# Bias loads and the tail of w1 in a two-layer attention and MLP kernel: plain DMAs in place of single elements, 768-byte runs in place of 256-byte ones, and a new table of priorities

## The chip, the cores and the metric

The kernel runs on one core of one Trainium2 chip. The metric is the device time of that core in microseconds (us). A profiled run also has a span, from its first to its last instruction, which is about 2 us shorter than the time; where this document divides a run into sections, they are sections of the span. Every run came with the mean clock that was granted to TensorE; 1.0 is full speed. In the views PE is TensorE, PEld its loading of weights, DVE is VectorE, ACT ScalarE, POOL GpSimd and SP SyncE; an arrow with a name says what an instruction waited for. A DMA is issued by an engine and lands later, when its data is there (b1's load in before: 2.00 us of issue on POOL, landed after 10.2).

## The reference

The program applies an attention mixer and an MLP twice over the same weights. There are 2048 tokens of 576 features, 32 heads of 18, a causal window of 256 keys, and 4608 hidden units.

```python
def _A_ref(x, wqkv, wo):                       # H = 32, Dh = 18, W = 256
    qkv = (x @ wqkv).reshape(B, S, 3, H, Dh)   # transposes cut
    q, k, v = qkv[0], qkv[1], qkv[2]
    scores = jnp.einsum("bhqd,bhkd->bhqk", q, k) * (Dh ** -0.5)
    # mask: key not after the query, and fewer than 256 before it
    p = _softmax(jnp.where(mask[None, None], scores, -1e9), axis=-1)
    return einsum("bhqk,bhkd->bhqd", p, v) ... @ wo

def _B_ref(x, w1, b1, w2, b2):
    y = _layernorm(x, axis=-1)
    h = _gelu(jnp.einsum("bsd,df->bsf", y, w1) + b1)
    return jnp.einsum("bsf,fd->bsd", h, w2) + b2

x = x + _A_ref(_layernorm(x), A_wqkv, A_wo)
x = x + _B_ref(_layernorm(x), B_w1, B_b1, B_w2, B_b2)
# ... and both lines once more
```

## The kernel before

The kernel does not issue instructions in the order of its text. Each operation is added as a task with an engine, what it reads and writes, and an estimated cost; a planner then fixes one order for each engine. A table of numbers by stage (`PL.nudge`) shifts the priorities of the planner. Tokens go in chunks of 512, four chunks in each of two layers. Attention of one chunk is interleaved with the MLP of the one before.

The biases, loaded by GpSimd (POOL) through the software queue:

```python
    b1col = sb("b1col", [P, NF], FP32)
    b2bc = sb("b2bc", [P, D], FP32)
    # ... cut ...
    dma("pool", b2bc[:, :], bass.AP(tensor=B_b2.tensor, offset=B_b2.offset, ap=[[0, P], [1, D]]), reads=["k3"], writes=["b2"], cls="b", ring=2,
        cost=1.0, prio=-1)

    def load_b1(e):
        src = bass.AP(tensor=B_b1.tensor, offset=B_b1.offset, ap=[[1, P], [P, NF], [1, 1]])
        with nc.allow_non_contiguous_dma(reason="bias column layout (init only)"):
            return e.dma_start(b1col[:, :], src)
    add("pool", load_b1, reads=["k3"], writes=["b1"], dma="b", ring=2, cost=2.0, lat=10.0, prio=-1)
```

The load of w1, one group of six column tiles at a time. Its contraction has 576 rows; the last 64 are split over the two halves of the partitions:

```python
        src = B_w1[512:576, cols].rearrange("p (a b f) -> p b a f", a=GS // 2, b=2)
        for b in range(2):
            dma("sp", w1_sb[64 * b:64 * b + 64, sl, 4 * GW:].rearrange("p (a f) -> p a f", a=GS // 2), src[:, b],
                writes=[f"w1b{sl}_{b}"], cls="w1", cost=0.6, lat=1.4, move=0.26, desc=192, prio=prio)
```

And two DMAs. One turns the normalised input of a chunk for the QKV products, on the SP queue; the other, on the POOL queue, brings the residual (the input that is added back later) of one chunk, 1152 KB at a time:

```python
        # in ln_norm_T
        add("sp", lambda e: e.dma_start_transpose(dst[:, :, i * 128:(i + 1) * 128], xn[:, sl, :]),
            reads=rd, writes=[f"{dname}{i}"], dma="t", ring=8, cost=1.3, lat=0.6, move=0.72, desc=640, prio=prio)
    # ... cut ...
    def x_load(a, cnt, reads, prio):
        dma("pool", x_res[:, a:a + cnt, :], x_dram[a * P:(a + cnt) * P, :].rearrange("(t p) d -> p t d", p=P), reads=reads,
            # ... cut ...
            cls="xr", ring=8, cost=1.2, prio=prio)
```

The softmax here doesn't subtract the row's maximum and nothing guards it: scores larger than these inputs give would overflow.

## Time and profile before

| | before |
|---|---|
| time, median of 3 runs | 926.46 us (925.78 to 926.63) |
| profiled run: time, span, granted clock | 925.61 us, 923.8 us, 0.998 |
| first mask of attention on POOL, in the profile | 21.60 us |
| load of the GELU table on ScalarE, ahead of the first MLP | 96.83 us |

The last two rows are milestones. I cut the span at them into a start, a middle and a rest, because the change touches the middle (the biases), all three (w1), and the order of the middle and the rest. For before these three are 21.60, 75.23 and 826.97 us.

The queues over the whole span (packets, MB, and time of packets as a share of 16 engines):

```profile
q1 hardware_dynamic: 212048, 119.90, 53.5%
q0 software_dynamic: 6880, 5.03, 2.9%
```

### The profile page before, as it was taken

What the parts mean: (1) busy time and instruction counts of PE and PEld (TensorE: products, weight loads), DVE (VectorE), ACT (ScalarE), POOL (GpSimd) and SP (SyncE); (2) the same over time, 40 slices, a digit from 0 to 9 for tenths busy, and PEclk for the clock granted to TensorE, in tenths of its full rate; (3) what the DMA queues carried; (4) which work ended last, traced back from release to release, by engine and by line L of the source; (5) the groups of instructions that cost most, each with busy time, mean ns of one, the idle gap of its engine ahead of it and who ended that gap; (6) DMA issues with size and microseconds to landing.
All of it is one profiled execution on the core that took longest, in us unless ns stands there. A gap on an engine that the chain in (4) does not pass through costs nothing. (4 is left out here: it accounts for less than half of the span.)

```text
span 923.8 us, 22403 instructions
## 1 busy us (share of the span) xinstructions
PE 898.5 (97%) x9370; PEld 567.3 (61%) x9408; DVE 319.3 (35%) x796; ACT 599.3 (65%) x721; POOL 372.8 (40%) x507
## 2 busy tenths in 40 slices
PE   8898999999999999999999999999999999999998
PEld 6566465565756657566565657666476665656556
DVE  5657113732317313184124521255123520241001
ACT  5877786677746777563665768646676777852441
POOL 3877353453505535062341644315443353610100
PEclk9999999999999999999999999999999999999999
DMA  7996819743197335852658351873619626175430
GB/s 196 163 226 121 217 57 263 159 138 117 29 244 137 119 114 134 180 103 56 193 77 258 55 192 40 225 142 64 199 40 212 154 71 202 44 201 158 145 116 27
DMA packets 221460, 129.01 MB, mean 140 GB/s; under 512 B 151856, under 2 KB 219184, under 8 KB 221360
## 3 DMA queue, kind: packets, MB, share of 16 engines
q1 hardware_dynamic: 212048, 119.90, 53.5%
q0 software_dynamic: 6880, 5.03, 2.9%
q10 hardware_dynamic: 2432, 2.65, 0.9%
q8 instruction: 74, 1.21, 0.6%
q14 instruction: 26, 0.21, 0.1%
HBM read 91.87 MB, written 2.36 MB: 102 GB/s over the span
## 5 line engine op out<-in xcount | busy, mean ns | idle before, releaser
L765 ACT ACTIVATE pT<-ps 128x1024 bf16<-128x1024 f32 (+2 forms) x384 | 349.3, 969 | 123.8 <-PE ps L756 122.8
L786 POOL TENSOR_SCALAR_AFFINE_SELECT pT<-pT 128x512 bf16<-128x512 bf16 (+1 forms) x368 | 281.7, 790 | 252.0 <-ACT pT L765 226.8
L920 PE MATMUL ps<-w_sb,hT 128*128 128x288 bf16 x2304 | 312.7, 286 | 1.9 <-DVE x_res L837 1.7
L894 ACT ACTIVATE hT<-ps,b1col 128x512 bf16<-128x512 f32 x288 | 198.0, 687 | 170.1 <-PE ps L891 170.1
L891 PE MATMUL ps<-xnTm,w_sb 128*128 128x512 bf16 x1114 | 256.4, 379 | 3.3 <-issue 1.9
L920 PEld LDWEIGHTS ps<-w_sb,hT 128*128 128x128 bf16 x2304 | 212.3, 98 | 74.1 <-issue 17.6
L891 PEld LDWEIGHTS ps<-xnTm,w_sb 128*128 128x128 bf16 x1152 | 108.7, 98 | 135.6 <-issue 17.0
L837 DVE TENSOR_TENSOR x_res<-ps,x_res 128x288 f32<-128x288 f32 x160 | 71.3, 450 | 262.6 <-PE ps L920 221.5
L670 PE MATMUL ps<-wqkv,xnTa 128*128 128x288 bf16 x960 | 136.8, 286 | 2.6 <-DVE qn L709 1.6
L803 PEld LDWEIGHTS ps<-vA,pT 128*128 128x128 bf16 x2880 | 95.1, 96 | 25.7 <-POOL pT L786 8.6
L670 PEld LDWEIGHTS ps<-wqkv,xnTa 128*128 128x128 bf16 x960 | 85.9, 97 | 37.0 <-issue 6.8
L803 PE MATMUL ps<-vA,pT 128*128 128x20 bf16 x2880 | 100.6, 171 | 4.2 <-POOL pT L786 3.3
L709 DVE CAST qn<-ps 128x288 bf16<-128x288 f32 x120 | 54.2, 455 | 100.8 <-PE ps L670 100.4
L902 POOL TENSOR_TENSOR x_res<-x_res,b2bc 128x576 f32<-128x576 f32 x32 | 44.9, 1402 | 104.9 <-ACT hT L894 104.8
L756 PE MATMUL ps<-qT,kT 32*128 32x384 bf16 (+2 forms) x1216 | 64.0, 276 | 3.0 <-ACT pT L765 2.0
L602 POOL TENSOR_SCALAR vtmp<-mv_all 128x1 f32<-128x1 f32 (+1 forms) x43 | 8.9, 207 | 130.8 <-DVE mv_all L593 129.2
L591 DVE BATCH_NORM_STATS2 st_all<-x_res 128x6 f32<-128x288 f32 x104 | 45.1, 449 | 9.3 <-DMA x_res<-in_A_x_dram 7.7
L696 DVE CAST vA<-ps 128x288 bf16<-128x288 f32 x64 | 29.0, 455 | 54.8 <-PE ps L670 54.7
L670 PE MATMUL ps<-wo_sb,attT 128*128 128x288 bf16 x320 | 46.9, 293 | 0.4 <-DMA attT<-attq 0.4
L813 DVE RECIPROCAL rinv<-ps 128x16 f32<-128x16 f32 x64 | 16.2, 254 | 85.0 <-PE ps L803 84.4
L879 PE MATMUL ps<-xnTm,w_sb 64*128 64x512 bf16 x288 | 39.5, 377 | 2.2 <-ACT hT L894 0.9
L614 DVE TENSOR_SCALAR xn<-x_res,mv_all,rstd 128x576 bf16<-128x576 f32 x52 | 36.7, 710 | 11.8 <-DMA xnTm<-xn 6.7
(42 smaller groups left out, 278.2 us busy)
## 6 DMA issues: line engine op xcount, KB each, us to landing
w_sb<-in_B_w_dram SPq DMA_DIRECT2D x48, 864.0 KB, 6.2
w_sb<-in_B_w_dram SPq DMA_DIRECT2D x48, 768.0 KB, 4.8
w_sb<-in_B_w_dram SPq DMA_DIRECT2D x96, 48.0 KB, 4.5
x_res<-in_A_x_dram POOLq DMA_DIRECT2D x4, 1152.0 KB, 8.7
out_dram<-xn SPq DMA_DIRECT2D x16, 144.0 KB, 1.8
wqkv<-in_A_wqkv_dram ACTq DMA_DIRECT2D x3, 576.0 KB, 7.2
hT<-in_A_x_dram SPq DMA_DIRECT2D x2, 576.0 KB, 5.0
wo_sb<-in_A_wo_dram ACTq DMA_DIRECT2D x1, 576.0 KB, 6.3
```

The costliest lines, as they stand in the source:

```text
L591: add("dve", lambda e, i=i, s=s: e.bn_stats(st_all[:, t, i, :], s[:, t, i * HB:(i + 1) * HB]), reads=res, writes=[f"st{t}_{i}"], cost=0.37 ...
L670: ins = e.matmul(bank(bs[o])[:, 0:HB], lhs(c), rhs(c, o * HB), start=(c == 0), stop=(c == KD - 1))
L709: add("dve", lambda e, b=bs[o], dst=dst: e.tensor_copy(dst, bank(b)[:, 0:HB].rearrange("p (h d) -> p h d", d=DH)), reads=[bs[o]], writes=[ ...
L756: ins = e.matmul(two(bs[j // 2])[:, j % 2, col:col + nq * 128], k_of(T0 + so)[0][32 * j:32 * j + 32, g, :], qs[32 * j:32 * j + 32, g, qo * ...
L765: add("act", lambda e, h2=h2: e.activation(pT[:, sl, 2 * h2:2 * h2 + 2, lo:hi], two(bs[h2])[:, :, lo:hi], ACT.Exp, scale=SCALE), reads=[bs ...
L786: add("pool", lambda e, ap=ap, pat=pat, sgn=sgn, kind=kind: e.affine_select(ap, ap, pattern=pat, compare_op=(ALU.is_ge if kind == "d" else ...
L803: ins = e.matmul(bank(B_O)[:, o:o + VW], pT[:, sl, j, col + qi * 128:col + (qi + 1) * 128], vA[:, (T0 + so) % VS, 4 * g + j, :], start=(fi ...
L837: add("dve", lambda e: e.tensor_tensor(x_res[:, t, sl], bank(b)[:, 0:HB], x_res[:, t, sl], ALU.add), reads=[b], writes=[f"x{t}h{hh}"], cos ...
L891: ins = e.matmul(bank(bk)[:, 0:n], w1_sb[:, sl, col:col + 128], xnTm[:, k % 2, c, 0:n], start=False, stop=(c == 3))
L894: add("act", lambda e, ff=ff, fl=fl, bk=bk: e.activation(hT[:, fl, 0:n], bank(bk)[:, 0:n], ACT.Gelu_apprx_tanh, bias=b1col[:, ff:ff + 1]), ...
L902: add("pool", lambda e, t=t: e.tensor_tensor(x_res[:, t, :], x_res[:, t, :], b2bc[:, :], ALU.add), reads=["b2", f"h{fl}"], writes=X(t), co ...
L920: ins = e.matmul(bank(b)[:, 0:HB], hT[:, fl, i * 128:(i + 1) * 128], w2_sb[:, fl, hh * HB:(hh + 1) * HB], start=(fl == 0), stop=(fl == NFH ...
```

## The change

The intent is to spare the DMA engines thousands of tiny packets. b1 comes as 36 rows of 256 bytes, is turned by one TensorE transpose, and is copied to fp32 by VectorE; b2 comes as a plain broadcast, in bf16, without a cast. Both move from POOL to SP. The last 64 rows of w1 come in runs of 768 bytes, where the first three and the last three column tiles take the place of the even and the odd ones. A new table of priorities goes with it.

```diff
-    PL.nudge = {"": -6.61, "ea0": -8.81, "eb0": -4.05, "q1.0": -40.73, ...      # cut
+    PL.nudge = {"b": 1.83, "ea0": -1.98, "ld0+": 40.46, "eb0": 2.23, ...        # cut
-    b2bc = sb("b2bc", [P, D], FP32)
+    b2bc = sb("b2bc", [P, D], BF16)
+    b1in = sb("b1in", [NF, P], BF16)
...
-        src = B_w1[512:576, cols].rearrange("p (a b f) -> p b a f", a=GS // 2, b=2)
         for b in range(2):
-            dma("sp", w1_sb[64 * b:64 * b + 64, sl, 4 * GW:].rearrange("p (a f) -> p a f", a=GS // 2), src[:, b],
-                writes=[f"w1b{sl}_{b}"], cls="w1", cost=0.6, lat=1.4, move=0.26, desc=192, prio=prio)
+            c0 = bb * GW + b * GW // 2
+            dma("sp", w1_sb[64 * b:64 * b + 64, sl, 4 * GW:], B_w1[512:576, c0:c0 + GW // 2], writes=[f"w1b{sl}_{b}"], cls="w1", cost=0.6,
+                lat=1.4, move=0.17, desc=64, prio=prio)
...
-                for ff, sl, bk in zip(fs, sls, bks):
-                    b = ff % 2
-                    col = 4 * GW + ff % GS // 2 * 128
+                for i in (0, 3, 1, 4, 2, 5):
+                    sl, bk = sls[i], bks[i]
+                    b = i // 3
+                    col = 4 * GW + i % 3 * 128
...
-    dma("pool", b2bc[:, :], ...)                                                # cut
-    add("pool", load_b1, reads=["k3"], writes=["b1"], dma="b", ...)             # cut
+    dma("sp", b1in[:, :], bass.AP(tensor=B_b1.tensor, offset=B_b1.offset, ap=[[P, NF], [1, P]]), reads=["k3"], writes=["b1i"], cls="b", ring=2,
+        cost=0.5, prio=-1)
+    dma("sp", b2bc[:, :], bass.AP(tensor=B_b2.tensor, offset=B_b2.offset, ap=[[0, P], [1, D]]), reads=["k3"], writes=["b2"], cls="b", ring=2,
+        cost=0.5, prio=-1)
+    add("pe", lambda e: e.transpose(bank(bb).bitcast(BF16)[:, 0:NF], b1in[:, :], ident[0:NF, 0:NF]), reads=["b1i", "ident"], writes=[bb],
+        cost=0.1, lat=0.22, prio=5, alloc=[bb])
+    add("dve", lambda e: e.tensor_copy(b1col[:, :], bank(bb).bitcast(BF16)[:, 0:NF]), reads=[bb], writes=["b1"], cost=0.1, lat=0.14, prio=5)
```

## The prediction

> **What bounds the kernel now.** I read the page's busy shares first, then the table of stretches (busy time of each engine between two times), then the waits by engine, and last the DMA view of the stretch in which the biases are loaded.
>
> The busy shares say which engine has no room:
>
> ```profile
> PE 898.5 (97%) x9370; PEld 567.3 (61%) x9408; DVE 319.3 (35%) x796; ACT 599.3 (65%) x721; POOL 372.8 (40%) x507
> ```
>
> TensorE (PE) works 898.5 of 923.8 us. Nothing in the change takes away a matmul of the layers, so whatever is gained has to come out of 923.8 - 898.5 = 25.3 us in which TensorE stands still, or from matmuls that run on a lowered clock. Where these lie is told by the stretches (columns: stretch and its length, then PE, PEld, DVE, ACT, POOL, each with its count of instructions, then granted clock, DMA share, GB/s):
>
> ```profile
> 0.00:20.00 20.00, 17.51 (x149) 13.20 (x150) 11.59 (x34) 8.67 (x14) 7.53 (x23) 1.00 0.86 216
> 20.00:30.00 10.00, 9.75 (x122) 7.18 (x119) 6.77 (x21) 8.29 (x12) 7.52 (x9) 1.00 0.65 127
> 30.00:40.00 10.00, 7.78 (x113) 4.77 (x114) 8.22 (x26) 8.61 (x13) 7.95 (x12) 1.00 1.73 106
> 40.00:65.00 25.00, 23.26 (x359) 15.38 (x363) 11.76 (x31) 20.92 (x29) 18.70 (x27) 1.00 1.25 235
> 75.00:90.00 15.00, 12.38 (x196) 8.00 (x189) 10.54 (x28) 12.20 (x14) 12.07 (x21) 0.89 0.61 138
> 100.00:900.00 800.00, 787.81 (x8017) 489.80 (x8053) 253.46 (x624) 523.87 (x625) 308.18 (x404) 1.00 0.54 139
> 900.00:923.80 23.80, 20.46 (x158) 15.17 (x155) 3.66 (x8) 4.13 (x6) 0.00 (x0) 1.00 0.08 26
> ```
>
> Subtract PE from the length of each row: 2.49 us idle in the first 20, 0.25 in the next 10, 2.22 in 30 to 40, 1.74 in 40 to 65, 2.62 in 75 to 90; 12.19 in the 800 us from 100 to 900, which is 1.5% of them; 3.34 at the end, nearly all of it after the last matmul (residual, output store, final barrier). In 75 to 90 the clock was 0.89, so there 0.11 x 15 = about 1.7 us more are lost inside busy time. The row 30 to 40 is the one with the most PE idleness per us outside the startup, and at the same time the one with the highest DMA share, 1.73, at only 106 GB/s.
>
> What TensorE waited for over the whole span is short (columns: waiting engine and line, what it waited for, us in total, times, longest):
>
> ```profile
> PE ps L756 <- ACT pT L765: 4.1, 11, 1.1
> PE ps L803 <- POOL pT L786: 3.3, 9, 0.6
> PE ps L891 <- issue: 1.9, 12, 0.2
> PE ps L920 <- DVE x_res L837: 1.7, 5, 0.6
> PE ps L670 <- DVE qn L709: 1.6, 4, 0.7
> ```
>
> The reader is to see what is missing: no wait of TensorE on w1, on the biases or on the weights of the MLP stands here. The longest are inside the attention loop (scores, exponential, mask, product with V) and are settled by the order that the scheduler gave to each engine.
>
> The DMA view of 30 to 40 us shows what fills the DMA engines there:
>
> ```profile
> q0 software_dynamic: 4624, 0.02, 101.6%
> q1 hardware_dynamic: 4205, 1.03, 70.9%
> xnTa<-xn SPq DMA_TRANSPOSE x2, 4.4
> ```
>
> q0 is the software queue: 4624 packets carry 0.02 MB. That is b1, 4608 single elements of two bytes[...], and by packet time it takes more than the share of everything else. The whole-span list of issues gives the usual landing of the same transpose, and what the biases themselves took:
>
> ```profile
> xnTa<-xn SPq DMA_TRANSPOSE x28, 2.6
> b2bc<-in_B_b_dram POOLq DMA_DIRECT2D x1, 288.0 KB, 5.7
> b1col<-in_B_b_dram POOLq DMA_DIRECT2D x1, 18.0 KB, 10.2
> ```
>
> [...] In the trace both bias loads are indeed on the software queue. [...] the w1 tail has runs of 256 B now and would have 768 B. No line of the before trace isolates the rate of these loads[...]; they land in 4.5 us, in a queue with the large loads. [...] The clock in the trace drops only around 75 to 90 us, where TensorE had also been idle for 2.62 us in pieces[...].
>
> **The change, part by part.**
>
> *Biases.* Removed: two DMA issues on POOL, 0.77 us (b2) and 2.00 us (b1) by the timeline, from 24.47 to 27.25 us. A mask instruction of POOL, whose exponential ended at 24.75 + 1.94 = 26.69 us, starts at 27.26, so the issue held it by about 0.57 us. Removed as well: 4624 + 144 software packets. Added: one load of 36 rows of 256 B, one broadcast load of 128 rows of 1152 B on SP, one transpose on TensorE (the present ones have a mean of 220 ns), one small copy on DVE (about 0.2 us by the smallest DVE rows), one PSUM bank for a moment. In the built order the transpose stands where the present trace is at about 37 us, while b1 is issued right after the x load of 24.18 us, which took 5.1 us to land: so I expect b1 there near 30 us and no wait at the transpose. First use of b1 is the first GELU at 98.9 us. Neither kernel waits for it.
>
> What this is worth: 30 to 40 has 2.22 us of idleness where the row before has 0.25, so at most about 2.0. The transposes of the next chunk's input, issued at 24.8 to 30.65 us, landed in 6.2 us (median in the stretch 20 to 30) rather than 2.6, which delays the Q of chunk 1; but the waits of the weight loads in 30 to 40 name the exponential first (1.7 us), then the mask (1.2) and the Q copy (0.8), so part of the idleness is of the attention loop and stays. I put the gain at half, 1.0 us. Less the transpose and two more warm-up matmuls in the order (46 against 44, these fill gaps): 0.2. Net 0.8.
>
> *w1's tail.* 96 loads of 192 runs of 256 B become 96 loads of 64 runs of 768 B: 18,432 packets become 6,144. The count of SP instructions stays, and so does the count of the half-height matmuls, which are only renumbered: even and odd column tiles become first three and last three, and the order 0, 3, 1, 4, 2, 5 still alternates upper and lower half. TensorE waits for no w1 load today, so from 100 us on this buys nothing directly. Six such loads are issued at 2.2 us, among the first x and QKV loads: 6 x 48 KB = 295 KB in a stretch that moves about 385 GB/s is 0.77 us of DMA time; if a fifth to a third of that goes, 0.15 to 0.25 us. I take 0.2.
>
> *The reordering.* The schedule is recomputed with another table of priorities. The order of TensorE differs in the middle chunks; the counts don't (2880, 2304, 1440, 960 and 320 of the large groups in both). Both tables look as if they had been searched for, so I expect the 12.19 us between 100 and 900 to move by about one or two us either way, and rather down, as a change is tuned after it is made: 0.8. The clock drop at 75 to 90 costs 1.7 us[...]; even odds that it is gone: 0.8.
>
> Sum: 0.8 + 0.2 + 0.8 + 0.8 = 2.6 us. From 926.46 that is 923.9. I shade it to 923.6, as the last two terms can overlap with a better fit at the start.
>
> **The rivals.** *A: DMA contention throughout.* The DMA share is 58% by the queues (53.5 + 2.9 + 0.9 + 1.1)[...]; if the transposes that feed the attention output and the MLP wait behind the w1 tail, 12,288 packets fewer would shorten every chunk. For it: the chain of waits has one transpose of 4.14 us at 628.43, and 630 to 635 has 0.98 us of PE idleness. Against: total PE waits on DMA are 0.4 us. It would make perhaps 919 to 920. *B: the order gets worse.* The bias loads now stand on SP between the x load and the transposes of chunk 1, in order; if the broadcast of b2 or a wait there holds the transposes, or the new order opens gaps in the attention loop and a second clock drop, the time is 927 to 929. For it: [...]four transposes follow each other without a pause from 24.80. Against: two issues of hardware DMAs are 0.4 to 0.6 us each. *C: nothing.* b1 was hidden anyway, and the idleness of 30 to 40 is all from the attention loop: 926.
>
> **Range and chances.** A small gain is the centre; A and a lucky reordering make the low end 919.0, B the high end 927.2. To be faster by over 2%, 18.5 us of the 25.3 idle ones would have to go, 3.3 of which are the fixed end: 1%. To be slower by over 2% a new stall in every chunk would be needed: 1%.
>
> **What would show it.** The software queue should fall to 2112 packets (four x loads of 528), the hardware queue from 212,048 to about 199,950; in 30 to 40 us PE should be busy near 8.8 of 10, and the landing of the chunk 1 transposes near 3 us; POOL should have no bias issue; the first 20 us should differ by less than 0.5; PE's idle time from 100 to 900 between 9 and 14 us; PE's busy sum within 3 us of 898.5. If 30 to 40 doesn't fill up, the contention step is wrong; if the gain lies after 100 us in waits on transposes, rival A was right; if it lies there with the DMA untouched, it was the order alone. A time under 919 or over 927.2 would make the prediction wrong.

The fraction behind the 0.2 ("a fifth to a third") and the even odds behind the last 0.8 were guesses of mine, which no trace shows. The 1.7 us of the clock are an estimate from the 0.89; in the trace the matmuls of the output projection took 371 ns in the mean from 75 to 90 us, 287 from 60 to 75 and from 100 to 200. b1's 4624 packets are 4608, one for each element, and 16 more, and what these 16 are is not shown. The issue of "0.4 to 0.6 us each" was 0.37 for the x load on SP in before; in after it is 0.51 for b1 and 0.58 for b2.

## The result and the profile after

| | before, same rounds | after |
|---|---|---|
| time, median of 4 runs | 926.55 us (925.78 to 927.32) | 925.61 us (925.06 to 926.65) |
| profiled run: time, span, clock | 925.61, 923.8, 0.998 | 925.06, 922.9, 1.0 |
| start, middle, rest of the span | 21.60, 75.23, 826.97 | 21.48, 74.51, 826.91 |

The ratio is 0.9991, with a 95% interval of 0.9974 to 1.0009: the same. A ratio here is taken from the fast runs of both kernels in the same rounds, so it is not quite the ratio of the medians in the table. The prediction, 923.6, was 2 us too low, and the time lies within its range.

The page of after begins with the busy shares, and its queues follow:

```profile
PE 901.4 (98%) x9411; PEld 566.0 (61%) x9411; DVE 317.0 (34%) x797; ACT 598.5 (65%) x721; POOL 365.5 (40%) x505
...
q1 hardware_dynamic: 199952, 120.06, 52.2%
q0 software_dynamic: 2112, 4.72, 2.0%
```

The intent was reached to the packet: 6880 - 2112 = 4768 software packets and 212,048 - 199,952 = 12,096 hardware packets are gone. The span is 0.9 us shorter. PE's busy sum rose by 2.9 us, but that is recording: the largest group of matmuls has 1114 records in before's trace and 1152 in after's, where the kernels have the same number of these matmuls (us busy, then the mean ns of one, then idle us just before):

```profile
L891 PE MATMUL ps<-xnTm,w_sb 128*128 128x512 bf16 x1114 | 256.4, 379 | 3.3 <-issue 1.9
```

```profile
L893 PE MATMUL ps<-xnTm,w_sb 128*128 128x512 bf16 x1152 | 260.5, 379 | 0.0
```

The first line is before's, the second is after's. The group alone is 4.1 us busier with its 38 records more, which is more than the whole sum rose by. Before's 3.3 us of idleness ahead of this group, where after has none, probably stand in the place of missing records. So PE's idleness from 100 to 900 us, 12.19 before and 800 - 791.61 = 8.39 after, has in truth moved by less than the two numbers say. Sums of PE can't settle a microsecond here; milestones can.

The stretches of after that answer to those of before (same columns: stretch, length, PE, PEld, DVE, ACT, POOL, clock, DMA share, GB/s):

```profile
0.00:20.00 20.00, 18.32 (x150) 13.89 (x151) 11.71 (x35) 8.58 (x14) 7.40 (x23) 1.00 0.83 217
30.00:40.00 10.00, 8.33 (x119) 5.02 (x120) 8.22 (x27) 8.24 (x13) 7.99 (x12) 1.00 0.62 101
75.00:90.00 15.00, 13.59 (x210) 9.64 (x207) 12.65 (x34) 10.17 (x11) 11.60 (x18) 1.00 0.75 115
90.00:100.00 10.00, 7.33 (x89) 4.36 (x88) 5.22 (x12) 7.13 (x8) 5.87 (x9) 1.00 0.92 138
100.00:900.00 800.00, 791.61 (x8084) 489.20 (x8083) 251.26 (x624) 523.72 (x627) 303.53 (x404) 1.00 0.54 139
```

The row of before that the prediction left out, and that matters now:

```profile
90.00:100.00 10.00, 9.84 (x142) 6.78 (x140) 6.29 (x15) 6.80 (x8) 6.01 (x9) 1.00 0.73 98
```

From 30 to 40 us the DMA share fell from 1.73 to 0.62, and PE gained only 0.55 of its 2.22 idle us. From 75 to 90 PE gained 1.21 us and the clock is whole. From 90 to 100 PE is busy 7.33 where it was 9.84, so 2.51 us went back. The waits of PE over the whole span name the cause (us in total, times, longest):

```profile
PE ps L757 <- ACT pT L766: 4.4, 13, 1.1
PE ps L804 <- POOL pT L787: 2.9, 7, 1.1
PE ps L671 <- DVE qn L710: 2.1, 5, 1.0
PE ps L881 <- DMA xnTm<-xn: 1.5, 1, 1.5
```

The fourth line is new. The timeline has it: the first MLP matmul waits for the last two transposes of its input, which the new order issues at 90.39 us.

```profile
90.39 4.33 SPq L635 DMA_TRANSPOSE xnTm<-xn  x2
...
97.56 0.82 PE L881 MATMUL ps<-xnTm,w_sb 64*128 64x512 bf16 x6 [1.54 <-DMA xnTm<-xn]
```

In before one of the four transposes of that tile goes at 78.65 us and the other three from 81.79 on, all issued by 92.46 us, and the first MLP matmul started at 97.08 without a wait:

```profile
81.79 10.67 SPq L634 DMA_TRANSPOSE xnTm<-xn  x3
...
97.08 0.82 PE L879 MATMUL ps<-xnTm,w_sb 64*128 64x512 bf16 x6
```

So what the new order won before 90 us it largely gives back by 98: the first MLP matmuls start at 97.56 us in after and at 97.08 in before. Part of it was not won at all but moved: the rest of after's 2.67 us of idleness from 90 to 100 is one wait of 1.13 us for an exponential, at 93.28, and before has a wait of the same length ahead of matmuls of the same form at 78.83.

### The profile page after: what moved, and what is told of

The parts are those of the page before. It is cut to its first block, busy times and chain, and to the rows that moved or that the text cites. A ratio compares the mean times of both kernels' runs of the same rounds, so it can differ in the third digit from the quotient of the medians.

```text
span 922.9 us, 22461 instructions
## 1 busy us (share of the span) xinstructions
PE 901.4 (98%) x9411; PEld 566.0 (61%) x9411; DVE 317.0 (34%) x797; ACT 598.5 (65%) x721; POOL 365.5 (40%) x505
## 3 DMA queue, kind: packets, MB, share of 16 engines
q1 hardware_dynamic: 199952, 120.06, 52.2%
q0 software_dynamic: 2112, 4.72, 2.0%
q8 instruction: 74, 1.21, 0.5%
## 5 line engine op out<-in xcount | busy, mean ns | idle before, releaser
L893 PE MATMUL ps<-xnTm,w_sb 128*128 128x512 bf16 x1152 | 260.5, 379 | 0.0
L671 PE MATMUL ps<-wqkv,xnTa 128*128 128x288 bf16 x960 | 134.5, 286 | 2.7 <-DVE qn L710 1.8
L904 POOL TENSOR_TENSOR x_res<-x_res,b2bc 128x576 f32<-128x576 f32 x32 | 40.8, 1275 | 115.7 <-ACT hT L896 115.6
L671 PE MATMUL ps<-wo_sb,attT 128*128 128x288 bf16 x320 | 45.0, 286 | 1.5 <-DMA attT<-attq 0.8
L757 PEld LDWEIGHTS ps<-qT,kT 32*128 32x128 bf16 x1216 | 19.5, 92 | 34.6 <-issue 18.4
```

The source lines that it names most:

```text
L671: ins = e.matmul(bank(bs[o])[:, 0:HB], lhs(c), rhs(c, o * HB), start=(c == 0), stop=(c == KD - 1))
L757: ins = e.matmul(two(bs[j // 2])[:, j % 2, col:col + nq * 128], k_of(T0 + so)[0][32 * j:32 * j + 32, g, :], qs[32 * j:32 * j + 32, g, qo * ...
L893: ins = e.matmul(bank(bk)[:, 0:n], w1_sb[:, sl, col:col + 128], xnTm[:, k % 2, c, 0:n], start=False, stop=(c == 3))
```

## The experiments

My theory after the first result had three parts. First, taking b1's packets away gains nothing in before's order, because what they slow is hidden there by the attention loop. Second, the w1 tail is worth some tenths of a microsecond. Third, the table of priorities fits the set of tasks it was made for, and its gains and losses cancel at the end. The rivals were that the packets were a cost of a microsecond or more which the new order threw away elsewhere, that w1's tail carried the gain, or that the two kernels differ in nothing but scatter.

Each batch of runs had its own runs of before beside it, eleven in each of the four batches.

### One part alone: the w1 tail

Before's kernel, with the new w1 tail and the new numbering of the half-height matmuls. The planner's estimates stay the old ones, so the order of every engine stays as it was.

```diff
-        src = B_w1[512:576, cols].rearrange(...)
+            c0 = bb * GW + b * GW // 2
-            dma("sp", w1_sb[64 * b:64 * b + 64, sl, 4 * GW:].rearrange(...), src[:, b], ..., move=0.26, desc=192, prio=prio)
+            dma("sp", w1_sb[64 * b:64 * b + 64, sl, 4 * GW:], B_w1[512:576, c0:c0 + GW // 2], ..., move=0.26, desc=192, prio=prio)
```

> Before with only the w1 tail changed (runs of 768 B, half-height matmuls renumbered), every instruction in the order of before. My theory (no engine waits for w1): within 0.5 us of before, 926.0 to 927.0, and the first real matmul of the start within 0.3 us. Rival A (DMA contention in every chunk): 12,288 packets fewer give 2 us or more, 924.5 or less. Hardware queue 199,760 packets in both theories.

Measured: correct, median 925.5 us (924.54 to 925.89, 6 runs) against 926.03 for before (924.85 to 934.35, 11 runs), ratio 0.9975 (0.9941 to 1.0009). The hardware queue has the expected 199,760 packets, and the time lies just under the 926.0 to 927.0 that I had expected. Start, middle and rest are 21.36, 75.36 and 826.68 us. Before's are 21.60, 75.23 and 826.97. The rest, which holds nearly all of the 96 loads, gained 0.29 us. The load itself lands no sooner in this kernel than in before (4.5 us in both):

```profile
w_sb<-in_B_w_dram SPq DMA_DIRECT2D x96, 48.0 KB, 4.5
```

So longer runs did not speed these loads up in any way that the landing shows.

### One part alone: fewer packets for b1

Before's kernel, with b1 read as 128 runs of 72 bytes. This puts the wrong bias into each place (the result: a relative error of 0.020), but keeps the load, its engine, its size and the order of all instructions, and takes away the single elements.

```diff
-        src = bass.AP(tensor=B_b1.tensor, offset=B_b1.offset, ap=[[1, P], [P, NF], [1, 1]])
+        src = bass.AP(tensor=B_b1.tensor, offset=B_b1.offset, ap=[[NF, P], [1, NF]])
```

> Before with b1 read in 128 runs of 72 B in place of 4608 single elements, order unchanged; its values land in wrong places on purpose, so the result is wrong. My theory: the contention at 25 to 37 us goes, PE gains 0.5 to 1 us there, and the start of the first GELU moves by 0 to 1 us; whole time 925.5 to 926.5. Rival C (hidden anyway): time as before, and 30 to 40 us keeps about 2.2 us of PE idleness. Software queue near 2,400 packets instead of 6,880.

Measured: median 925.93 us (925.0 to 927.84), ratio 0.9982 (0.9948 to 1.0017), on the same chip and beside the same runs of before as the last one. The packets are gone, as the DMA views of this kernel from 30 to 40 us and from 20 to 30 us show:

```profile
q0 software_dynamic: 242, 0.21, 9.3%
...
xnTa<-xn SPq DMA_TRANSPOSE x2, 6.0
b1col<-in_B_b_dram POOLq DMA_DIRECT2D x1, 18.0 KB, 5.9
```

q0's share fell from 101.6% to 9.3%, and b1 lands in 5.9 us rather than 10.2. This run's start is 2 us late, so the stretch that answers to 30 to 40 us of before, counted from the first mask, is 32.08 to 42.08:

```profile
32.08:42.08 10.00, 7.78 (x110) 4.76 (x110) 8.11 (x25) 8.51 (x13) 7.85 (x12) 1.00 0.57 108
```

The DMA share is 0.57 where it was 1.73, and PE is busy 7.78 us, to the digit what it was. The middle is 75.38 us, where before's is 75.23. In these profiles of before's order the 4608 single elements cost TensorE nothing.

They did slow the transposes down. The two of chunk 1 with 6.0 us above are only the first two, as the window ends at 30 us. Here are all four, in order: before, this run, a run told below that has the new w1 tail as well, and after:

```profile
DMA to landing us min/median/max: 5.9/6.2/7.1
DMA to landing us min/median/max: 3.2/4.8/6.3
DMA to landing us min/median/max: 2.6/3.7/6.1
DMA to landing us min/median/max: 2.6/3.5/4.9
```

By the single landings in the traces, with few packets for b1 the first transpose still takes over 6 us, and the last 3.2 and 2.6, where before's last takes 6.2. So the late landing of the later transposes does go with b1's elements, as the prediction had said; what is missing is an engine that waits for it. The first one has something else ahead of it in the first three kernels:

```profile
b2bc<-in_B_b_dram POOLq DMA_DIRECT2D x1, 288.0 KB, 5.7
```

```profile
b2bc<-in_B_b_dram SPq DMA_DIRECT2D x1, 144.0 KB, 3.9
```

In before, and in this run, the software load of b2, 288 KB, is issued on POOL 0.33 us ahead of the first of these transposes (24.47 and 24.80 us in before). In after (second line) b2 is issued behind the first three, and the first lands in 4.9 us. No run moved b2 alone, so that b2 slows the first one is not shown.

The profiled run had a late start, which is told here because it comes up again. An input load of 576 KB, issued at 12.77 us, took 6.7 us to land, and VectorE, whose next instruction needed it, waited:

```profile
19.45 0.82 DVE L591 BATCH_NORM_STATS2 st_all<-hT 128x6 f32<-128x288 bf16 x2 [2.91 <-DMA hT<-in_A_x_dram]
```

In before's profile the same load landed in 4.8 us and the wait was 0.8. The first mask moved from 21.60 to 23.68 us by it. Neither part of the change is near, so this is scatter that both kernels have, and alone it is larger than what is being looked for.

### The tables exchanged

Before's kernel with after's table of priorities, and after's with before's.

```diff
-    PL.nudge = {"": -6.61, "ea0": -8.81, ...
+    PL.nudge = {"b": 1.83, "ea0": -1.98, "ld0+": 40.46, ...
```

> Before with only the new table of priorities. If the order made the difference: 925 to 926, as the changed kernel. My theory: a table is fitted to one set of tasks and the schedule is chaotic, so on other tasks it is no better or worse: 926 to 929. If the loads made the difference: 926.5.

> The changed kernel with the old table of priorities. If loads and layout are the gain, 925.6 stays or nearly; my theory: the parts are worth under 1 us and the misfit of the table costs 1 to 3 us: 926 to 929.

Measured: before with the new table 941.49 us (938.25 to 947.53), ratio 1.0161 (1.0118 to 1.0204); after with the old table 931.38 us (930.84 to 933.01), ratio 1.0043 (1.0008 to 1.0078). Both give correct results. These are the only two differences whose interval leaves out 1. The waits of PE in the first of them:

```profile
PE ps L756 <- ACT pT L765: 7.4, 18, 1.1
PE ps L879 <- ACT pT L765: 4.8, 3, 2.1
PE ps L803 <- POOL pT L786: 4.7, 14, 1.4
```

No DMA is named. The attention loop itself is worse arranged, and MLP matmuls wait behind exponentials (4.8 us, a wait that before doesn't have). The clock has a share in it too (0.991 over the run, where before's profiled run had 0.998): it was 0.55 from 205 to 220 us of this profile and 0.89 from 260 to 275, where before's stayed at 1.00 from 100 to 900. By PE's busy 9.89 and 12.59 us in these two stretches that is, as an estimate, 0.45 x 9.89 + 0.11 x 12.59 = about 6 of the 15 us. Start, middle and rest are 21.61, 73.07 and 841.7 us: the middle is the best of all kernels and the rest is 15 us longer. A table is fitted to one set of tasks; on another it can cost far more than the change of the tasks is worth.

### After again, and before with w1's tail nearly gone

The second batch, on another chip. After is unchanged. In the other kernel, before with only 1 of 64 rows of each tail loaded from the fourth group on. The other rows keep older values of w1, wrong; the outputs stayed within the tolerance all the same, so the check of the result says nothing here.

```diff
+        nr = 64 if B < NB1 else 1
-            dma("sp", w1_sb[64 * b:64 * b + 64, sl, 4 * GW:]..., src[:, b],
+            dma("sp", w1_sb[64 * b:64 * b + nr, sl, 4 * GW:]..., src[0:nr, b],
```

> The changed kernel once more, with more rounds beside before, to settle the size of the difference. My theory: 0.3 to 1.2 us faster than before in the same rounds (ratio 0.9987 to 0.9997), so the order and the parts together are worth under 1.5 us. Rival: the 0.9 us of the first comparison was scatter of the start, and the two are the same within 0.3 us.

> Before in its own order, where after the first three groups each w1 tail load moves only one row of each half (768 B each) instead of 64, so the result is wrong on purpose. It bounds what any w1 tail layout can give. My theory: no wait hangs on these loads, so 925.3 to 926.3, at most 0.5 us better than before. Rival A: 3 us or more better, since nearly all their packets are gone. Packets of the hardware queue near 195,000.

Measured: after 927.05 us (923.81 to 928.47), before in the same rounds 926.2 (924.1 to 933.4), ratio 0.9982 (0.995 to 1.0015). The medians point one way and the means the other, because two of before's eleven runs took over 932 us. Before without the tail: 927.08 us (925.06 to 932.13, 8 runs), ratio 0.9981 (0.9947 to 1.0015).

The sections of the second kernel decide about w1: 22.43, 81.13 and 826.74 us. The rest is 0.23 us shorter than before's 826.97, with nearly all of the tail's bytes gone. By this profile no shape of these loads could give more from there on. A check on the scatter: the rest is 826.68 to 826.81 us in the three profiles that have a changed tail in before's order, and 826.94 to 827.35 in the four without (before, fewer packets for b1, and two runs below). So a few tenths are plausible, and not more. The middle, on the other hand, is 5.9 us longer than before's, which the next runs put down to something other than w1. After's own sections in this batch are 22.33, 74.07 and 828.6: its rest is 1.7 us longer than in its first profile, so its order is no better than before's from 96 us on.

### Three times b1, and both parts in before's order

The first has b1's element-wise load two times more, into space of w2 that is not yet in use; POOL issues two more DMAs. The second joins the first two experiments: the new w1 tail and b1 in 128 runs, in before's order (wrong, relative error 0.020 as before).

```diff
+    for r in range(2):
+        def more(e, r=r):                      # b1's element-wise load again, into w2_sb
+            ...
+        add("pool", more, reads=["k3"], writes=[f"w2s{r}"], dma="bx", ring=2, cost=0.0, lat=0.0, prio=-1)
```

> Before with the element-wise b1 load issued three times (the copies go to space of w2 that is not yet in use), 9,248 software packets more. If the contention of b1 costs time, it grows with the dose: my theory of the prediction (1 us for one) gives plus 2 us or more, 928 and up. Rival C (hidden): within 1 us of before, and what there is comes from the 2 us of issue on POOL for each, ahead of the masks.

> Before in its own order with both the w1 tail in 768-byte runs and b1 in 128 runs (b1's values in wrong places on purpose). If the parts are worth anything, it shows here without a new order: my theory 0.2 to 0.8 us better than before, 925.2 to 925.8 if before is at 926. Rival (all of the gain is the order): equal to before within 0.2 us.

Measured: three times b1 930.36 us (928.27 to 935.18), ratio 1.0033 (0.9996 to 1.007). The dose gave 928 and up, as the contention theory had said, but its profile does not give it to the packets. POOL's two added issues take 3.64 us from 30.07 on, and TensorE then stands for the mask behind them:

```profile
35.05 0.47 PE L803 MATMUL ps<-vA,pT 128*128 128x20 bf16 x12 [2.61 <-POOL pT L786]
```

Before has no wait for a mask over 0.4 us there. From 35 to 40 us the clock was 0.50 (five QKV matmuls took 1.38 us at 37.73, and 0.79 at 41.94). This is the other half of rival C, the time of issue ahead of the masks, so the run does not isolate the packets.

Both parts together gave 930.33 us (925.18 to 932.34), ratio 1.0014 (0.9975 to 1.0052), with two runs near 925 and four from 929 to 932. Two harmless parts had together become slow, which none of my theories allowed. The profiled run of the pair was one of the slow ones, 22.38, 80.31 and 826.81 us: again all of it in the middle. Its DMA view and timeline from 38 to 50 us:

```profile
xnTa<-xn SPq DMA_TRANSPOSE x1, 6.6
...
41.00 0.82 POOL L535 DMA_DIRECT2D x_res<-in_A_x_dram  x1
41.13 1.20 SPq L634 DMA_TRANSPOSE xnTa<-xn  x1
47.74 2.58 PE L670 MATMUL ps<-wqkv,xnTa 128*128 128x288 bf16 x10 [3.51 <-DMA xnTa<-xn]
```

And the same two issues in before's profile:

```profile
39.65 1.21 SPq L634 DMA_TRANSPOSE xnTa<-xn  x1
40.49 0.83 POOL L535 DMA_DIRECT2D x_res<-in_A_x_dram  x1
```

In before the transpose goes 0.84 us ahead of the load of 1152 KB and lands in 2.6 us. In the slow run it goes 0.13 us behind it and lands in 6.6, and TensorE waits 3.5 us for it. So the transpose on SP took 4.0 us more behind the load on POOL than ahead of it.

The clock was lower there too. The rows are of the pair, from 45 to 55 us:

```profile
45.00:50.00 5.00, 2.26 (x10) 1.35 (x10) 0.46 (x1) 0.00 (x0) 1.11 (x2) 0.70 1.35 299
50.00:55.00 5.00, 4.74 (x54) 2.53 (x53) 2.00 (x5) 3.20 (x4) 2.00 (x3) 0.62 0.19 37
```

The wait of 3.51 us ends at 47.74, and the clock was 0.70 and 0.62 in these two stretches, where before had 1.00 in both. The matmuls took longer as well: the ten behind the wait 2.58 us, where five of the same shape took 0.79 at 43.12. By the clock 0.30 x 5 + 0.38 x 5 = 3.4 us of full-speed time are missing in these two rows, as an estimate, about as much again as the wait. That the wait brought the lower clock is not shown. Wait and clock make 6.9 us; less the 1.7 of before's dip from 75 to 90, which this run does not have, that is 5.2, and the middle is 5.1 longer.

In before's order, and in after's own, the profiles sort by this race (a margin is the start of the load's issue less that of the transpose's; three times b1 has two POOL issues more than before's order). The last row, a run told further below, does not:

| kernel | margin, us | transpose lands, us | middle, us |
|---|---|---|---|
| before | +0.84 | 2.6 | 75.23 |
| new w1 tail | +0.84 | 2.5 | 75.36 |
| b1 in few packets | +0.84 | 2.6 | 75.38 |
| both parts | -0.13 | 6.6 | 80.31 |
| w1 tail nearly gone | -0.60 | 6.4 | 81.13 |
| three times b1 | -0.13 | 7.1 | 83.97 |
| after | +0.50 | 2.6 | 74.51 |
| after again | +0.50 | 2.6 | 74.07 |
| after with the two old loads | +0.39 | 6.3 | 77.39 |

Of the three slow profiles only that of both parts shows the race alone. Three times b1 had lost the 2.61 us above before it, and with w1's tail nearly gone the clock was already 0.71 and 0.61 in 40 to 42.5 and 42.5 to 45 us (five QKV matmuls took 1.25 us at 40.86 and 1.38 at 43.00, but 0.79 at 38.47), ahead of its wait of 2.49 us at 48.62. What made the transpose late against the load in these two runs is not shown.

Before itself had 8 runs of 48 at 929 us and above, up to 934.35. None of those has a trace here; that they lost this race too is an inference from the kernels with its order, only weakly backed by their clocks, which were 0.994 to 0.998, as fast runs of before have 0.996 to 1.0. After had no such run in 10. With 8 in 48, ten runs without one have a chance of (40/48) to the tenth, 16%, so a missing tail is not shown.

### The load of the residual moved behind two masks

If the race is the cause, a later load should take the slow runs away. In both kernels I moved the first such load behind the next two mask instructions of POOL, after the planner had fixed the order.

```diff
+        at = next(i for i, (st, t) in enumerate(order) if t.dma == "xr")
+        load = order.pop(at)
+        masks = [i for i, (st, t) in enumerate(order) if i >= at and t.eng == "pool"]
+        order.insert(masks[1] + 1, load)
```

> Before with one instruction moved: the first 1152 KB load of x_res stands two masks later on POOL; all else keeps its place. New theory: the runs of before at 928 to 934 us are those in which this load is issued ahead of the transpose of xn for the next chunk, which then lands after 6 to 7 us instead of 2.6 and makes TensorE wait 2.5 to 4 us[...]. With the load later that race can't be lost: every run at or under 927.5, median 925.5 to 926.5, no wait of TensorE on that transpose. Rival (the scatter is from the chip or from elsewhere in the first 100 us): runs of 928 us and more go on in about a quarter of the cases, as in before.

> The changed kernel with the same move. It was not seen to lose the race in ten runs (its highest 928.5), so by the new theory little changes: 924.5 to 926.5, the spread a bit less. By the rival it keeps 923.8 to 928.5.

Measured: before so changed 927.95 us (925.5 to 929.67), against 926.08 (925.39 to 933.31) in the same rounds, ratio 1.0009 (0.9984 to 1.0034); after so changed 925.75 us (924.45 to 927.28), ratio 0.9985 (0.9959 to 1.0011). The transpose landed in 2.6 us in both, with a margin of about 2 us, and no run of before reached 930. But I had expected before to lie under 927.5, and it does not. In its profile the middle is 75.65 and the rest 827.02, as ever; the start is 25.23 us, 3.6 later than before's. That is the late input load again, landing in 6.6 us:

```profile
DVE st_all L595 <- DMA hT<-in_A_x_dram: 2.8, 1, 2.8
```

By the sign that I had set, 928 us and more in about a quarter of the runs, the rival came out: three of before's six runs so changed were at 928.16 or more, one of the eleven beside them. So the profiles show what losing the race costs. That it is the cause of before's slow runs is not shown: the time has no gain, and six runs without one over 930 have a chance of about (40/48) to the sixth, 33%, anyway. In after the later load has 21.43, 75.40 and 828.07 us, no gain either.

### A search for a better table

After's tasks with the later load, and a table found by random search over the planner's own plan.

> The changed kernel's loads with another table of priorities, found by a random search over the scheduler's own plan, and with the move of the x_res load: the attempt at a version better than both. If the order is what sets the time, 922 to 925; if the tables have reached what the chip gives, 925 to 927 like the others. A regression over 928 would say that the plan no longer tells orders apart at this level.

Measured: 928.46 us (925.97 to 933.13), ratio 1.0021 (0.9992 to 1.0051). The rest is the shortest of all, 824.99 us, 2 us under before's; the middle, 79.09, gives back 4. Three of its six runs took 929 to 933 us although the load stands later, 2.4 us behind the transpose in the profile, so these slow runs need some other cause. It is no better version, and I have none: no kernel is shown to beat both.

### The two software loads put back into after

The converse of the second experiment: after unchanged, and besides its own bias loads the two old ones, added on POOL in their old place, into space not yet in use. Nothing reads them. Nothing else moves in the order; POOL has two issues more.

```diff
+    for r in range(2):                         # r = 0: b2, broadcast with a cast; r = 1: b1, element by element
+        add("pool", lambda e, r=r: again(e, r), reads=["k3"], writes=[f"w2s{r}"], dma="bx", ring=2, cost=0.0, lat=0.0, prio=-1)
```

> The changed kernel with its own order, to which the two old software bias loads are added again (into space of w2 that is not in use yet, nobody waits for them), so that POOL's issue time and the 4,768 packets return and nothing else. If their removal gave what the change gave: 0.5 to 1.5 us over the changed kernel, 926 to 927.5, and runs over 929 as before has them. If the order gave it: 924.5 to 927 with the mean within 0.5 us of the changed kernel's ten runs (926.1), no run over 929, and the clock at 1.0 in every run. In the trace 30 to 40 us should fall from 8.3 to about 7.8 us of PE work either way.

Measured: 928.29 us (926.03 to 930.25), ratio 1.0012 (0.9985 to 1.0038) against before's 925.77 in the same rounds. The mean, 928.31, is 2.2 us above the mean of after's ten runs, 926.12, on other chips; with the scatter of both this is good to about 1.6. Against the means of before in the same rounds it is 1.5 us above, where after was 0.8 and 1.4 below. The profile has the loss where one would look for it, in the middle: 22.31, 77.39 and 828.5 us, where after had 74.51 and 74.07. From 20 to 30 us the DMA view of this kernel has the slow landing back:

```profile
xnTa<-xn SPq DMA_TRANSPOSE x3, 6.3
```

And TensorE waits for it, over the span:

```profile
PE ps L671 <- DMA xnTa<-xn: 2.8, 2, 2.0
```

The timeline gives the two places: 0.82 us at 32.46, for chunk 1's transpose, and 1.95 at 48.10, for chunk 2's, which went 0.39 us ahead of the residual load (41.79 and 42.18) and landed in 6.3 us nonetheless. By the ends of the two issues, 42.99 and 43.01, they were level, where after had 0.27 us between them and before 0.46. From 30 to 40 us the clock was 0.83, where after had 1.00. So by these runs and this profile the old loads cost 2 to 3 us in after's order, although b1's elements cost nothing in before's. That b2's load cost nothing there was not tested.

## Why the prediction was right or wrong

**The whole.** Predicted were 923.6 us and 98% for the same; measured were 925.61 at first and 927.05 in a second batch, and the same. The centre was 2 us too low at first; the first profile has 0.9 of the 2.6 us that I had summed.

**The biases (0.8).** The mechanism was right for the DMA engines and failed at its last link. The transposes of chunk 1 did land late beside b1's elements: the median is 6.2 us in before, 4.8 and 3.7 in the two runs with few packets for b1, 3.5 in after. The step that failed is that this "delays the Q of chunk 1". TensorE does not wait for these transposes in before's order: in the stretch that answers to 30 to 40 us PE was busy 7.78 us with the elements and 7.78 without them, and the middle was 75.23 and 75.38. So rival C, nothing because it was hidden anyway, was right for that order. Where a profile has TensorE waiting for chunk 1, the wait ends with the first transpose (0.17 to 1.14 us in five profiles), so what the elements do to the later ones stayed hidden throughout. After's order does not hide the two loads as a pair: with them back TensorE waits 0.82 us for chunk 1 and 1.95 for chunk 2, and there the pair is worth about 2.2 us by the runs and 2.9 to 3.3 by the middle. The size 0.8 lies between, and is the right number of neither. The checks came out: 2112 software packets, 3.2 us for the transposes, no bias issue on POOL, PE 8.33 of 10 from 30 to 40 us (8.77 in the second profile; 8.8 was predicted). The last is no sign of the elements, as the run without them kept 7.78.

**w1's tail (0.2).** Measured 0.29 us in the rest with the new tail and 0.23 with nearly none of it. The size was right, by luck, as its fraction was a guess. The argument took it from the start and said that the loads buy nothing directly from 100 us on. The start is where it can't be seen: it scatters by 3.6 us from a load that is the same in both. Rival A, contention throughout, is refuted, since all of the tail's bytes were worth no more than that. (In its sum of shares the last term should be 0.6 + 0.1, not 1.1; the 58% stands.)

**The reordering (0.8), and a change "tuned after it is made".** This step failed. The rest is 826.91 and 828.6 us in after's two profiles and 826.97 in before's: between nothing and 1.6 us worse (828.07 and 828.5 in two more profiles of after's order with other changes). PE idleness from 100 to 900 us, 8.39, fell just below the range of 9 to 14 that I gave, but through records that before's trace lacks. The table is tuned in the sense that it fits this set of tasks (the exchange cost 15 and 5 us); it was not tuned to beat the old pair. Rival B, a worse order, was right in a small way: the transposes for the first MLP come late.

**The clock (0.8).** The even odds came out on the good side: the dip from 75 to 90 us is gone, and all of after's 10 runs had a mean clock of 1.0, while only 15 of the 44 runs of before in the four batches did. But I counted it as time at the end, and it isn't. What is won up to 90 us, 1.21 us of PE time and the whole clock, meets 2.51 us more of idleness from 90 to 100, where the first MLP matmul waits 1.54 us for its transposes and an earlier one 1.13 for an exponential. The milestone at 96 us has moved by 0.84 us in all, start included.

**First 20 us.** I said less than 0.5 us of difference; PE differs by 0.81 (18.32 for 17.51). That is warm-up matmuls, which fill gaps; the first mask is at 21.60 and 21.48 us, so in progress the check holds.

**What stays open.** Whether after is faster by a microsecond or not at all: the medians favour it in the first batch and before in the second. Why after kept its margin of 0.50 us in both profiles, where three of the kernels with before's order kept 0.84 and three lost it. Whether before's slow runs are that race, as none has a trace here and moving the load did not take them away. And whether b2's software load makes the first transpose behind it land late, by its size, its cast or its place on POOL.

## What to carry to other kernels

A share of DMA packets, even 101.6% of a stretch, need not cost time: in before's order b1's elements made transposes late (6.2 us for 4.8), but TensorE did not wait for these, and the middle was 75.23 us with the elements and 75.38 without. So look for an engine on the path that waits for a transfer in that stretch, and take the packets away alone, in the same order, before crediting them with a gain. When a tuned order goes with a change, exchange the orders first: here that moved the time by 5 and 15 us, while the change moved it by one or none. And where two queues issue a small transfer that is awaited and a large one that isn't within a microsecond of each other, look at which goes first in slow and fast runs (here the small one landed in 2.5 to 2.6 us when ahead by 0.50 us or more, and in 6.4 to 7.1 behind); compare by milestones, since whole runs hid the effect in a scatter from elsewhere. Before reading a median of landings in a window, see that the window holds the same DMAs in both runs: here a start 2 us later left the two quick ones out.

## What these traces show of the hardware

- A DMA transpose of 128 x 640 bf16 landed in 2.5 to 2.6 us where it was issued 0.50 us or more ahead of a load of 1152 KB on another queue, in 6.4 to 7.1 us behind that load, and in 6.3 when it was only 0.39 us ahead.
- Runs of 256 and of 768 bytes landed alike in this kernel, 4.5 us for 48 KB, and the rest of the span was 826.97 and 826.68 us. The loads stand in a queue with larger ones, so the rate of such a load alone is not shown; the length of the runs made no difference here.
- In before's profile the clock was 0.89 from 75 to 90 us, where the longest single wait of TensorE was 1.13 us and its idleness 2.62 us in pieces. In the pair's, it was 0.70 and 0.62 in the two stretches of 5 us in and after a wait of 3.51 us. In the profile with w1's tail nearly gone it was 0.71 and 0.61 before the wait of 2.49 us. What lowers it is not shown.
- One input load scatters from run to run: 576 KB issued at the same place landed in 4.3 to 6.7 us in these profiles, and the first mask came up to 3.6 us later where it was late.
- Four transposes landed in 6.2 us in the median beside the 4608 elements of b1, and in 4.8 beside 128 runs of the same 18 KB.
